# Trading the places of two weight loads in GpSimd's order, and dropping seven multiplied zero blocks

## The chip, the cores and the metric

The kernel runs on one core of one Trainium2 chip. The metric is the device time of one execution in microseconds (us), taken as the median of several runs. Engines are called as the profile calls them: PE (TensorE, matrix products), PEld (its weight loads), DVE (VectorE), ACT (ScalarE), POOL (GpSimd) and SP (SyncE, which here only issues DMAs).

## The reference, cut to what matters

```python
# attention: batch 4, 8 heads, 768 steps, head width 48
f = 1.0 / (1.0 + np.exp(-f_logit))
for t in range(S):
    state = f[:, :, t, :, None] * state + np.einsum('bhd,bhe->bhde', k[:, :, t], v[:, :, t])
    y[:, :, t] = np.einsum('bhd,bhde->bhe', q[:, :, t], state)
# its output, 3072 tokens of width 384, goes through a gated block of width 1536
gate = np.maximum(x @ w_gate, 0.0)
val = x @ w_val
return (gate * val @ w_out).astype(np.float32)
```

The inputs q, k, v, f_logit and the three weight matrices are f32; the output is f32.

## The kernel before

The recurrence is computed in chunks of 128 steps, six chunks for each of four batch entries. For a chunk, ACT makes exp and log of f_logit (`ef`, lines 478 and `ln`, 481), PE forms running sums of the logs (`cum`, lines 494 to 506), ACT turns those into factors (`ek` and `eq`, lines 516 and 518), and POOL or DVE multiply k and q with them (`hk`, `hq`, line 540). PE then makes the masked scores (`s`, line 650 in the first chunks; DVE masks them in `m`, line 657), the output of the chunk (`y`, line 672, and `yi`, line 708) and the new state (`kv`, line 695). ACT or DVE copy the output to `xT` (line 597), from where the gated block takes it: `g` and `u` (line 792) are the products with one slice of 128 columns of w_gate and of w_val, `r` (lines 797 and 798) is the maximum with 0, `p` (line 800) the product of both, and `o` (line 813) the product with w_out.

The weights come from memory as f32 and are cast to bf16 by DMAs that POOL issues (line 431). They come in slices: `wg2+2` holds columns 2 and 3 of w_gate (in units of 128 columns, called j), `wg0+2` columns 0 and 1, `wg4+4` and `wg8+4` four columns each; `wv...` the same of w_val, `wo...` row blocks of w_out. A two-column slice of w_gate or w_val has 384 rows of 1 KB in memory; `wo0+2` has 128 rows of 3 KB. The inputs q, k, v and f_logit are loaded by DMAs that SP and ACT issue (lines 406 and 411).

Every operation has a number. The table `ORDER` lists, by hand, for each engine the numbers in the order in which it issues them; each engine works strictly in that order, and waits for others by semaphores. Names such as `g00.1` mean operation `g`, chunk 0, batch place 0, slice 1; `cum13` is the running sum of chunk 1, place 3. Around the change these stand in the orders:

- PE: ... cum10 (232), cum11 (243), a filling, g00.1 (150), u00.1 (152), g00.0 (146), y02 (138), cum13 (279), cum12 (268), yi03 (142), u00.2 (156) ...
- POOL: ... hk01 (90), hq01 (91), wo0+2 (70), wv0+2 (52), sd10 (108), v02 (122), hq02 (117), hq03 (127), wg0+2 (51), wv2+2 (57), wg4+4 (62), wv4+4 (63) ...
- ACT: ... ef10, ln10, ef12 (266), r00.3 (159), ek10, eq11, dc10, eq10, r00.2 (155), ek11, ln12 (267), r00.0 (147), x02 (141), ek12 ...
- DVE: ... m031, sd11, m030, m020, m021 (135), r00.1 (151), p00.1 (153), x03 ...

An entry `~7512` in PE's list is a filling: 7 products of a zero tile, each 512 columns wide, whose results are overwritten (line 877). The number 60100 stands for 60 of width 100, and so on. A filling is written to the PSUM bank that the next operation opens, so that the wait for that bank's earlier reader (here r00.3 on ACT) stands ahead of the filling.

`HELD` gives some DMAs a wait that the data do not ask for: an entry `a: b` lets the load with number a start only when the load with number b has landed. Number 50 is `f0.2` (f_logit of the second unit of chunk 0), 53 is `k0.2`, 58 is `f1.0`. The waits for g00.1 are r00.3 (its PSUM bank) and the landing of wg0+2; for u00.1, m030 (its bank) and wv0+2; for g00.0, m020 (its bank); for y02, m021 and r00.2; for cum13, ln12; for o02.0, the first user of w_out, wo0+2 and wo2+2.

Of the kernel before, what the change touches and what calls it, by code (L numbers as in the profile page):

```python
# [22 lines left out]
ORDER = {  # L23
    "PE": [
        45, ~60100, 76, 87, ~4512, 84, ~3512, 92, 82, 103, ~2512, 94, 123, 112, 97, ~7512, 120, ~2512, 130, 102, 128, 106,
        118, 139, 158, 133, 154, 232, 243, ~7512, 150, 152, 146, 138, 279, 268, 142, 156, 160, 148, 174, 176, 170, 172, 186,
# [37 lines left out]
    ],  # L64
    "POOL": [
# [4 lines left out]
    ],  # L70
# [6 lines left out]
}  # L77

HELD = {
    51: 53, 57: 58, 59: 63, 63: 58, 65: 69, 67: 71, 70: 50, 71: 60, 72: 54, 517: 68,  # L80
}

BANKS = [
# [859 lines left out]
```

## Time and profile before

| | |
|---|---|
| median of 3 runs | 194.01 us (193.71 to 194.05) |
| the profiled execution: its own time | 193.82 us |
| its span, first to last instruction | 192.0 us |
| PE busy | 185.4 us |
| DVE busy | 146.3 us |
| ACT busy | 83.3 us |
| POOL busy | 59.8 us |
| granted clock of PE | 1.00 |

The span is the time between the first and the last instruction; the execution's own time has 1.8 us more around it. A row of a timeline gives the start, the duration, the engine, the source line, the operation and its tiles, how many instructions are merged in it, and in brackets how long the engine had been idle and what it then waited for. Instructions of one engine are pipelined, so the next one often starts a little before the duration of the one ahead is over. In a view of the DMA queues, q1 is the queue that SP fills and q0 the one that POOL fills; the columns are packets, megabytes and the time that the packets took as a share of the 16 DMA engines in that stretch. "DMA to landing" is the time from a DMA's issue until its last part has landed.

### The profile page before, as it was taken

The numbers are of one execution on the slowest core, as the hardware profiler recorded it, in microseconds if no ns is written. First come the engines' busy times: TensorE is split into PE (matmuls) and PEld (weight loads), VectorE is DVE, ScalarE is ACT, GpSimd is POOL, SyncE is SP. The second block draws the span as 40 slices with busy tenths as digits, with TensorE's granted clock in tenths as the row PEclk, the third lists the DMA queues.
The fourth block names the chain that finished last, engine by engine and source line by source line (L and its number), as shares of the span: only waits on it lengthen the run. The fifth ranks groups of instructions, "written<-read, shape, count | busy, mean of one in ns | idle before, by whom it ended". The sixth has DMA issues, their size and how long they took to land.

```text
span 192.0 us, 4872 instructions
## 1 busy us (share of the span) xinstructions
PE 185.4 (97%) x1992; PEld 110.1 (57%) x2010; DVE 146.3 (76%) x264; ACT 83.3 (43%) x183; POOL 59.8 (31%) x92
## 2 busy tenths in 40 slices
PE   7989999999999999999999999999999999999994
PEld 7556675565645556655555755556555555555553
DVE  4569946999868989879986789996888947677331
ACT  2776954520387780472214896613351220222211
POOL 8899320301055830358200273911180000000000
DMA  5999999999989997999989997991337010000413
GB/s 147 325 283 252 211 205 279 214 223 279 229 183 199 214 226 149 234 196 242 216 187 225 246 223 169 228 177 31 71 106 199 15 41 3 2 0 0 164 43 124
DMA packets 110311, 32.44 MB, mean 169 GB/s; under 512 B 103504, under 2 KB 110032, under 8 KB 110288
## 3 DMA queue, kind: packets, MB, share of 16 engines
q1 hardware_dynamic: 95120, 25.44, 59.7%
q0 software_dynamic: 3776, 3.54, 11.3%
q10 hardware_dynamic: 11392, 3.15, 7.2%
q8 instruction: 16, 0.26, 0.6%
q14 instruction: 7, 0.06, 0.1%
HBM read 25.95 MB, written 4.72 MB: 160 GB/s over the span
## 4 chain that ended last, share of the span: by engine, by line
PE 83%; DVE 5%; DMA 4%; ACT 3%; issue 1%; POOL 1%; SPq 1%; ACTq 0%
PE ps L792 43%; PE ps L813 25%; DMA f_in<-in_f_logit_dram 4%; PE ps L584 2%; DVE gT L800 2%; PE ps L745 2%; DVE hats L541 2%; PE ps L672 1%; PE ps L503 1%; PE ps L494 1%; POOL hats L540 1%; PE ps L772 1%; PE ps L650 1%; PE ps L756 1%; DVE qkT L556 1%
## 5 line engine op out<-in xcount | busy, mean ns | idle before, releaser
L800 DVE TENSOR_TENSOR gT<-relu,ps 128x512 bf16<-128x512 bf16 (+1 forms) x76 | 48.5, 655 | 15.4 <-PE ps L792 11.4
L792 PE MATMUL ps<-xT,wv 128*128 128x512 bf16 (+1 forms) x225 | 57.0, 368 | 0.3
L792 PE MATMUL ps<-xT,wg 128*128 128x512 bf16 (+1 forms) x216 | 55.2, 367 | 0.7 <-issue 0.2
L813 PE MATMUL ps<-wo,gT 128*128 128x384 bf16 (+2 forms) x300 | 51.9, 320 | 0.2 <-DVE gT L800 0.2
L797 ACT ACTIVATE relu<-ps 128x512 bf16<-128x512 f32 (+1 forms) x39 | 21.8, 565 | 48.5 <-PE ps L792 27.5
L813 PEld LDWEIGHTS ps<-wo,gT 128*128 128x128 bf16 x300 | 27.1, 98 | 18.4 <-DVE gT L800 1.2
L792 PEld LDWEIGHTS ps<-xT,wv 128*128 128x128 bf16 x228 | 23.6, 108 | 19.7 <-ACT expo L518 0.3
L792 PEld LDWEIGHTS ps<-xT,wg 128*128 128x128 bf16 x228 | 23.3, 108 | 18.8 <-ACT xT L597 0.3
L798 DVE TENSOR_SCALAR relu<-ps 128x512 bf16<-128x512 f32 (+1 forms) x37 | 24.9, 674 | 5.8 <-PE ps L792 4.8
L570 POOL CAST vpad<-v_in 128x384 bf16<-128x384 f32 x14 | 7.5, 549 | 43.7 <-PE ps L745 22.6
L592 DVE TENSOR_TENSOR ptm<-ps,tri 128x512 bf16<-128x512 f32 x32 | 19.9, 682 | 1.3 <-PE ps L584 1.3
L540 POOL TENSOR_TENSOR hats<-q_in,expo 128x384 bf16<-128x384 f32 x14 | 14.5, 1044 | 9.6 <-ACT expo L518 9.1
L540 POOL TENSOR_TENSOR hats<-k_in,expo 128x384 bf16<-128x384 f32 x13 | 13.8, 1071 | 6.5 <-ACT expo L516 3.7
L478 ACT ACTIVATE f_in<-f_in 128x768 f32<-128x768 f32 x12 | 10.1, 844 | 11.4 <-DMA f_in<-in_f_logit_dram 11.4
L456 POOL TENSOR_TENSOR st<-ssum,dec 128x384 bf16<-128x384 f32 x11 | 9.7, 878 | 17.1 <-DVE ssum L454 17.0
L518 ACT ACTIVATE expo<-ps 128x384 f32<-128x384 f32 x24 | 11.7, 491 | 4.1 <-PE ps L503 2.9
L597 ACT ACTIVATE xT<-ps 128x384 bf16<-128x384 f32 x10 | 5.4, 549 | 17.9 <-PE ps L672 8.6
L516 ACT ACTIVATE expo<-ps 128x384 f32<-128x384 f32 x24 | 11.5, 493 | 1.1 <-PE ps L494 0.6
L819 ACT ACTIVATE osb<-ps 128x384 f32<-128x384 f32 (+1 forms) x15 | 7.3, 484 | 10.4 <-PE ps L813 10.3
L877 PE MATMUL ps<-zeros 128*128 128x100 bf16 (+1 forms) x82 | 10.9, 311 | 0.4 <-issue 0.2
L657 DVE TENSOR_TENSOR ptm<-ps,tmask 128x512 bf16<-128x512 f32 x16 | 10.2, 682 | 1.4 <-PE ps L650 1.4
L481 ACT ACTIVATE bneg<-f_in 128x768 bf16<-128x768 f32 x12 | 10.1, 842 | 0.2
(78 smaller groups left out, 169.3 us busy)
## 6 DMA issues: line engine op xcount, KB each, us to landing
out_dram<-osb SPq DMA_DIRECT2D x23, 192.0 KB, 2.8
f_in<-in_f_logit_dram SPq DMA_DIRECT2D x11, 384.0 KB, 6.0
k_in<-in_k_dram SPq DMA_DIRECT2D x11, 384.0 KB, 5.6
q_in<-in_q_dram SPq DMA_DIRECT2D x10, 384.0 KB, 5.7
v_in<-in_v_dram SPq DMA_DIRECT2D x8, 384.0 KB, 4.9
v_in<-in_v_dram ACTq DMA_DIRECT2D x4, 384.0 KB, 6.1
q_in<-in_q_dram ACTq DMA_DIRECT2D x2, 384.0 KB, 7.1
wg<-in_moe_w_gate_dram POOLq DMA_DIRECT2D x2, 384.0 KB, 9.1
```

Of the source, the lines that this page charges most:

```text
L478: add(f"ef{c}{b0}", by("ACT", lambda: sc.activation(raw, raw, AF.Exp, scale=-1.0), act_(n)), keys, keys, key=P)
L516: add(f"ek{c}{b}", by("ACT", lambda: sc.activation(ex[:, 1, :], bc.ap[:, 0:HD], AF.Exp, scale=1.0), act_(HD)), [bc], [f"expk{ei}"], key=P + 1)
L518: add(f"eq{c}{b}", by("ACT", lambda: sc.activation(ex[:, 0, :], bc.ap[:, 0:HD], AF.Exp, scale=-1.0), act_(HD)), [bc], [f"expq{ei}"], key=P ...
L540: return {**by("POOL", lambda: gp.tensor_tensor(o, i_, e_, ALU.mult), pool_(HD)), **by("DVE", lambda: ve.tensor_tensor(o, i_, e_, ALU.mult ...
L592: add(f"m{c}{b}{j}", by("DVE", lambda b=b, j=j, mi=mi: ve.tensor_tensor(ptm[mi][:, j, :, :], s[b, j].ap[:, :].rearrange("p (n t) -> p n t" ...
L657: add(f"m{c}{b2[i]}{j}", by("DVE", lambda i=i, j=j, mask=mask: ve.tensor_tensor(ptm[mi[i]][:, j, :, :], s[j, i].ap[:, :].rearrange("p (n t ...
L792: z = te.matmul(bank.ap[:, 0:n], wt[:, kt, w_cols(j)], xT[xi][:, kt, n0:n1], start=(kt == 0), stop=(kt == NK - 1))
L797: add(f"r{c}{b0}.{j}", {**by("ACT", lambda: sc.activation(rdst, gate.ap[:, 0:n], AF.Relu), act_(n)), **by("DVE", lambda: ve.tensor_scalar_ ...
L798: **by("DVE", lambda: ve.tensor_scalar_max(rdst, gate.ap[:, 0:n], 0.0), dve_(n))}, [gate], [f"relu{ri}"], key=P)
L800: add(f"p{c}{b0}.{j}", by("DVE", lambda: ve.tensor_tensor(gT[gi][:, j, n0:n1], rdst, val.ap[:, 0:n], ALU.mult), dve_(n)), [val, f"relu{ri} ...
L813: z = te.matmul(o.ap[:, 0:e1 - e0], gT[gi][:, j, b * C:(b + 1) * C], wo[:, j, e0:e1], start=(j == 0), stop=(j == NJ - 1))
L877: te.matmul((op.opens[0].ap if op.opens else banks[7])[:, 0:fill % 1000], zeros[:, 0:128], zeros[:, 0:fill % 1000], start=True, stop=True, ...
```

## The change

Two numbers trade places in POOL's list, 70 (`wo0+2`) and 51 (`wg0+2`), and so do their entries in `HELD`: what is issued early waits for f0.2, what is issued late waits for k0.2, as before, but now it is wg0+2 that is issued early and wo0+2 that is issued late. The filling `~7512` ahead of 150 (`g00.1`) is taken out of PE's list. All other orders, waits and data are the same; g00.1 keeps its waits for r00.3 and for wg0+2.

```diff
 ORDER = {
     "PE": [
...
-        118, 139, 158, 133, 154, 232, 243, ~7512, 150, 152, 146, 138, 279, 268, 142, 156, 160, 148, 174, 176, 170, 172, 186,
+        118, 139, 158, 133, 154, 232, 243, 150, 152, 146, 138, 279, 268, 142, 156, 160, 148, 174, 176, 170, 172, 186,
...
     "POOL": [
-        25, 1, 36, 37, 38, 2, 4, 34, 11, 5, 20, 13, 7, 14, 8, 33, 26, 3, 39, 35, 16, 41, 17, 56, 40, 90, 91, 70, 52, 108,
-        122, 117, 127, 51, 57, 62, 63, 69, 68, 273, 71, 72, 73, 278, 264, 428, 420, 300, 392, 384, 395, 405, 393, 425, 418,
+        25, 1, 36, 37, 38, 2, 4, 34, 11, 5, 20, 13, 7, 14, 8, 33, 26, 3, 39, 35, 16, 41, 17, 56, 40, 90, 91, 51, 52, 108,
+        122, 117, 127, 70, 57, 62, 63, 69, 68, 273, 71, 72, 73, 278, 264, 428, 420, 300, 392, 384, 395, 405, 393, 425, 418,
...
 HELD = {
-    51: 53, 57: 58, 59: 63, 63: 58, 65: 69, 67: 71, 70: 50, 71: 60, 72: 54, 517: 68,
+    70: 53, 57: 58, 59: 63, 63: 58, 65: 69, 67: 71, 51: 50, 71: 60, 72: 54, 517: 68,
 }
```

## The prediction

> **What bounds the kernel now.** The page comes first: how full PE is, and which engine the chain that ended last runs through.
>
> ```profile
> span 192.0 us, 4872 instructions
> PE 185.4 (97%) x1992; PEld 110.1 (57%) x2010; DVE 146.3 (76%) x264; ACT 83.3 (43%) x183; POOL 59.8 (31%) x92
> PE 83%; DVE 5%; DMA 4%; ACT 3%; issue 1%; POOL 1%; SPq 1%; ACTq 0%
> ```
>
> PE sets the end, so whatever shortens PE's list shortens the kernel, provided that nothing else takes the place. The second view is the chain of waits in order of time, around the filling.
>
> ```profile
> 21.05 0.15 issue
> 21.20 1.46 PE ps L877 x6
> 22.66 0.98 PE ps L792 x9
> 23.64 0.66 PE ps L672 x62
> ```
>
> The filling (L877; six of its seven products are recorded) takes 1.46 us of the chain. Then PE works without a gap: g00.1, u00.1, g00.0 (nine products), y02 (L672). So at most 1.46 us can be won. Third, PE's own timeline there, with an earlier row (12.22) that shows how soon PE follows ACT:
>
> ```profile
> 12.22 0.82 PE L494 MATMUL ps<-bneg,tsum 128*128 128x384 bf16 x4 [0.20 <-ACT bneg L481]
> ...
> 22.49 0.49 PE L792 MATMUL ps<-xT,wg 128*128 128x256 bf16 x3
> 22.82 0.49 PE L792 MATMUL ps<-xT,wv 128*128 128x256 bf16 x3
> 23.15 0.49 PE L792 MATMUL ps<-xT,wg 128*128 128x256 bf16 x3
> 23.57 0.73 PE L672 MATMUL ps<-ptm,vpad 64*32 64x128 bf16 x64
> 24.24 0.82 PE L494 MATMUL ps<-bneg,tsum 128*128 128x384 bf16 x4
> ```
>
> Fourth, the two engines that feed these steps. First ACT's timeline (the row at 11.33 belongs to the earlier example), then DVE's.
>
> ```profile
> 11.33 0.83 ACT L481 ACTIVATE bneg<-f_in 128x768 bf16<-128x768 f32 x1
> ...
> 19.80 0.84 ACT L478 ACTIVATE f_in<-f_in 128x768 f32<-128x768 f32 x1 [0.40 <-DMA f_in<-in_f_logit_dram]
> 20.55 0.37 ACT L797 ACTIVATE relu<-ps 128x256 bf16<-128x256 f32 x1
> ...
> 22.32 0.38 ACT L797 ACTIVATE relu<-ps 128x256 bf16<-128x256 f32 x1
> 22.58 0.50 ACT L516 ACTIVATE expo<-ps 128x384 f32<-128x384 f32 x1
> 22.95 0.85 ACT L481 ACTIVATE bneg<-f_in 128x768 bf16<-128x768 f32 x1
> 23.69 0.39 ACT L797 ACTIVATE relu<-ps 128x256 bf16<-128x256 f32 x1
> 24.36 0.60 ACT L597 ACTIVATE xT<-ps 128x384 bf16<-128x384 f32 x1 [0.28 <-PE ps L672]
> ```
>
> ```profile
> 20.88 1.88 DVE L657 TENSOR_TENSOR ptm<-ps,tmask 128x512 bf16<-128x512 f32 x3
> ```
>
> This is the view that matters most. From 19.80 on ACT runs without a break until 24.08 (23.69 + 0.39): ef12, r00.3, the factors, r00.2, ek11, ln12, r00.0. Only its start is outside its own list: the landing of f1.2 at 19.80. And ln12, which ends at 22.95 + 0.85 = 23.80, is what cum13 needs; in the kernel before PE comes to cum13 at 24.24 and finds it ready. ACT is thus 0.4 us behind the filling, hidden by it.
>
> **The change part by part.** *The wait for wg0+2.* These rows give its issue, its landing and POOL's timeline:
>
> ```profile
> L431 POOL DMA_DIRECT2D wg<-in_moe_w_gate_dram x1: 815/815/815, 16.0 to 16.0; - x1
> ...
> DMA to landing us min/median/max: 6.0/6.0/6.0
> ```
>
> ```profile
> 11.17 0.59 POOL L431 DMA_DIRECT2D wo<-in_moe_w_out_dram  x1
> 11.76 0.75 POOL L431 DMA_DIRECT2D wv<-in_moe_w_val_dram  x1
> ...
> 14.12 1.95 POOL L540 TENSOR_TENSOR hats<-q_in,expo 128x384 bf16<-128x384 f32 x2 [0.30 <-ACT expo L518]
> 16.01 0.81 POOL L431 DMA_DIRECT2D wg<-in_moe_w_gate_dram  x1
> ```
>
> It lands at 16.0 + 6.0 = 22.0, and the filling covers that. Issued at 11.17 instead, it lands at 17.2, and has 4 us to spare until 21.2. That wait is gone.
>
> *The cost on POOL.* Issuing wg takes 0.81 us against 0.59 us for wo, so everything up to hq02 comes 0.22 us later; hq02 had 0.30 us of idle time ahead of it, waiting for ACT. Cost nothing, with 0.08 us to spare; without that cover, it would push the two `hq` that PE's transposes wait for by 0.22 us at most. After 16.01 the later weight loads are issued 0.22 us sooner, which nothing on PE waits for. wo0+2, now issued at 16.0, has until the first product with w_out:
>
> ```profile
> 41.33 0.81 PE L813 MATMUL ps<-wo,gT 128*128 128x384 bf16 x4
> ```
>
> *What PE meets without the filling.* r00.3 ends at 20.92 and g00.1 starts where the filling did, 21.20, done 0.33 us later (22.49 to 22.82). The three masks end about 21.5, 22.1 and 22.76 (20.88 + 1.88, in thirds). u00.1 needs the first: about 21.6. g00.0 needs the second: about 22.2. y02 needs the third: about 22.85, and it takes 0.67 us (23.57 to 24.24), to 23.52. Then cum13 needs ln12: 23.80 and the 0.06 us that PE followed ACT by at 12.22 (11.33 + 0.83 = 12.16), so 23.86 instead of 24.24. So even if nothing else moved, of 1.46 us only 0.38 us remain: the stall goes from the zeros to the masks (some 0.6 us in two waits) and to ln12 (0.34 us).
>
> *What the new order does to f1.2.* The 384 rows of wg0+2, where wo0+2 has 128, now go out on q0 beside f1.2, whose landing starts ACT's run. Here are its landing (the maximum is f1.2: 10.2 + 9.6 = 19.8) and the DMA queues in four stretches: 14 to 16 us (wo0+2 on q0), its part 14.5 to 15, 16 to 18 (wv0+2) and 18 to 19 (q1 nearly alone).
>
> ```profile
> L406 SPq DMA_DIRECT2D f_in<-in_f_logit_dram x2: 2096/2219/2342, 7.8 to 10.2; - x2
> ...
> DMA to landing us min/median/max: 8.6/9.1/9.6
> ```
>
> ```profile
> q1 hardware_dynamic: 876, 0.33, 62.1%
> q0 software_dynamic: 141, 0.19, 52.5%
> ...
> q1 hardware_dynamic: 240, 0.09, 64.6%
> q0 software_dynamic: 34, 0.05, 57.2%
> ...
> q0 software_dynamic: 391, 0.20, 71.2%
> q1 hardware_dynamic: 601, 0.23, 56.6%
> ...
> q1 hardware_dynamic: 828, 0.31, 113.6%
> ```
>
> Alone, q1 moves 828 packets in 1 us. Beside wo0+2 it moved 876 in 2 us, so the slice cost it (1656 - 876) / 828 = 0.94 us. Beside wv0+2 it moved 601: (1656 - 601) / 828 = 1.27 us. wg0+2 has the same rows as wv0+2, so exchanging it for wo0+2 ahead of f1.2 costs f1.2 about 0.33 us. The bounds: 0, since both slices write the same amount (0.19 and 0.20 MB in these stretches); and 0.48 us, if wo's price is scaled from the half microsecond in which it alone was on q0: (414 - 240) / 828 = 0.21 us for 34 of its 128 packets, 0.79 us for all, and 1.27 - 0.79 = 0.48. A gain isn't excluded either, and is rival C. I take 0.33, because the whole of both slices is in it.
>
> [...]
>
> *The sum.* f1.2 lands at 20.13, ACT's run moves with it, ln12 ends at 24.13, cum13 starts at 24.19 instead of 24.24: a gain of 0.05 us. With the bounds: cum13 at 23.86 to 24.34, a gain of 0.38 to a loss of 0.10. From there PE's list is as before and goes on as before, so the shift is carried to the end. The profiled execution took 193.82 us, 1.82 us more than its span; it becomes 193.77. The median of the runs is 0.19 above it, 194.01, and becomes 193.96.
>
> **The rivals.**
> - B, f1.2 doesn't move: 0.38 us less, 193.63. For it: equal bytes. Against it: 601 packets against 876.
> - C, f1.2 comes earlier: the wg slice takes 0.22 us longer to issue, so its packets may start later and let f1.2's pass; ACT then isn't what PE waits for, and y02 behind the third mask is. cum13 follows y02 at 23.52: 0.72 us less, 193.29. Against it: wo's first packets are there in the stretch 14.5 to 15, when f1.0, ahead of f1.2 on the same queue, hadn't landed yet (7.8 + 8.6 = 16.4), so much more than 0.22 us is needed.
> - The change does what its words say, the zeros' 1.46 us all come back: 192.55. Against it stand the masks and ln12, which no part of the change touches.
> - D, slower: f1.2's last part comes much later than the packet count says. It decides from 0.77 us on (0.38 us of room and 0.39 for a slowdown that can be told), and every tenth beyond is a tenth at the end: 1.0 us late gives 24.86 for cum13, 194.63. For it: the two f loads issued one behind the other took 8.6 and 9.6 us, so a landing can be a microsecond off. Against: the upper bound of 0.48.
> - E, slower: the zeros kept PE busy, and without them the clock falls. The rows of windows (PE busy is the second number with its count, the clock comes after POOL's):
>
> ```profile
> 12.00:12.50 0.50, 0.30 (x3) 0.21 (x3) 0.50 (x2) 0.17 (x1) 0.50 (x1) 1.00 1.31 200
> 21.00:24.30 3.30, 3.15 (x81) 2.12 (x82) 2.60 (x5) 3.06 (x9) 0.00 (x0) 1.00 1.28 204
> ```
>
>  [...] Against it: at 12 us PE stood at 0.30 of 0.50 with the clock at 1.00, and the new waits are 0.1 to 0.4 us each, with work between them. [...]
>
> **How the numbers follow.** The forecast, f1.2 some 0.2 to 0.5 us late and the gain eaten, has 0.52. B has 0.16, C 0.12, the full gain 0.02, D 0.12, E 0.06. What can be told from no change is about 0.2%, 0.39 us. C and the full gain are faster, and of B, which stands at that line, 0.05: 0.19. D and E are slower: 0.18. The rest, 0.63, is no difference. The predicted time is 194.0. The range goes down to C with a little for the runs' spread, 193.2, and up to D at 1.0 us late, 194.6; it leaves out E and the full gain. The forecast's own range is 193.6 to 194.2.
>
> **What would show it right or wrong.** Right: no L877 rows near 21; ACT's row of ef12 at about 20.1, still behind its DMA; cum13's row between 24.1 and 24.3, released by ACT's bneg. ef12 at 19.8 and cum13 at 23.86 is B; cum13 directly behind y02 at 23.5 is C; a clock under 1.00 is E. The step that I trust least is the 0.33 us: it is inferred from stretches with different neighbours, and if the landing of f1.2 follows something else than the packets ahead of it, the forecast is wrong by that.

## The result, and the profile after

| | time (median) | runs | ratio to the kernel before, 95% interval |
|---|---|---|---|
| kernel before | 193.94 us | 6 | |
| changed kernel | 195.02 us (194.77 to 195.22) | 6 | 1.0055 [1.0044, 1.0066] |

The change costs 1.08 us. The page of the changed kernel: its span, its engines, the packets of kind "instruction", and the chain by engine.

```profile
span 193.1 us, 4877 instructions
PE 185.7 (96%) x2003; PEld 109.1 (56%) x2003; DVE 146.2 (76%) x264; ACT 83.3 (43%) x183; POOL 60.2 (31%) x92
q8 instruction: 16, 0.26, 0.6%
PE 79%; DMA 5%; DVE 5%; SPq 5%; ACT 4%; issue 2%; ACTq 0%
```

"issue" is time in which an engine waited for nothing that the profile shows. Its step from 1% to 2% of the chain is little more than rounding (1.4% before, 1.5% after); what counts is one new piece of 1.14 us, which follows below. First, however, the place of the change. PE's timeline of the changed kernel around g00.1 (21.17), u00.1, g00.0, y02 (22.96) and cum13 (24.06):

```profile
21.17 0.50 PE L792 MATMUL ps<-xT,wg 128*128 128x256 bf16 x3
21.68 0.51 PE L792 MATMUL ps<-xT,wv 128*128 128x256 bf16 x3
22.28 0.50 PE L792 MATMUL ps<-xT,wg 128*128 128x256 bf16 x3
22.96 0.88 PE L672 MATMUL ps<-ptm,vpad 64*32 64x128 bf16 x64 [0.18 <-ACT relu L797]
24.06 0.82 PE L494 MATMUL ps<-bneg,tsum 128*128 128x384 bf16 x4 [0.21 <-ACT bneg L481]
```

And ACT's timeline of it, ef12 and ln12:

```profile
20.00 0.84 ACT L478 ACTIVATE f_in<-f_in 128x768 f32<-128x768 f32 x1 [0.53 <-DMA f_in<-in_f_logit_dram]
...
23.15 0.85 ACT L481 ACTIVATE bneg<-f_in 128x768 bf16<-128x768 f32 x1
```

Here all went much as foreseen: the wait for wg0+2 is gone, f1.2 lands 0.20 us later, ACT's unbroken run moves with it, and cum13 follows ln12 at 24.06, 0.18 us earlier than before. PE keeps this lead for 26 us. It loses it at one place, in yi13 (L708). PE's timeline there, the changed kernel and then the kernel before:

```profile
49.19 1.47 PE L813 MATMUL ps<-wo,gT 128*128 128x384 bf16 x8
50.59 0.29 PE L708 MATMUL ps<-qkT,st 128*32 128x128 bf16 x8
52.02 0.24 PE L708 MATMUL ps<-qkT,st 128*32 128x128 bf16 x4 [1.14 <-issue]
52.20 0.51 PE L695 MATMUL ps<-vpad,hats 64*128 64x96 bf16 x16
```

```profile
49.37 1.47 PE L813 MATMUL ps<-wo,gT 128*128 128x384 bf16 x8
50.78 0.35 PE L708 MATMUL ps<-qkT,st 128*32 128x128 bf16 x12
51.06 0.51 PE L695 MATMUL ps<-vpad,hats 64*128 64x96 bf16 x16
```

Before, yi13's twelve products run in one piece. Now eight run, then PE stands still for 1.14 us, and then the other four run, in the middle of one operation whose only wait lies ahead of its first product. The lead of 0.19 us (50.78 - 50.59) is a lag of 1.14 us (52.20 - 51.06) behind it: 1.33 us lost. The lag is still 1.1 us at the end (193.1 - 192.0). The windows view of 50.6 to 52.1 shows that no other engine was at work that PE could have waited for: DVE is busy for 0.14 us of it, ACT and POOL not at all; the changed kernel first, then the kernel before (the columns are the length, then PE, PEld, DVE, ACT and POOL busy, the clock, the DMA share and GB/s):

```profile
50.60:52.10 1.50, 0.36 (x13) 0.19 (x12) 0.14 (x1) 0.00 (x0) 0.00 (x0) 1.00 1.26 271
```

```profile
50.60:52.10 1.50, 1.50 (x34) 0.85 (x32) 0.81 (x2) 0.73 (x2) 0.00 (x0) 1.00 1.23 312
```

The clock stands at 1.00. What did happen just ahead of the gap stands in the view of the DMA queues: an "instruction" packet of 16 KB, the fifth of the sixteen. In the changed kernel it starts in the stretch 49 to 50.6 us, beside a busy queue q10; in the kernel before the packet of the same number starts in 45.5 to 47 us, beside busy queues too (q1 92.4%, q10 31.1%).

```profile
q10 hardware_dynamic: 1771, 0.34, 132.4%
q8 instruction: 1, 0.02, 5.1%
```

```profile
q8 instruction: 1, 0.02, 5.4%
```

Either packet took 1.3 us (5.1% of 16 engines in 1.6 us, 5.4% in 1.5 us): it was not slower in the changed kernel, it came later, at 49.39 instead of 46.71 us.

So the first theory, F, which this profile doesn't show and the runs below test: these packets bring PE's program, in blocks of 16 KB. The zeros were not only 1.46 us of work but also fourteen instructions, seven products and seven weight loads. Without them, by F, all of PE's later code lies fourteen instructions sooner with respect to the blocks, and one block is asked for so late that PE runs out of instructions in yi13.

### The profile page after: what moved, and what is told of

Same layout as the page of the kernel before. It is cut to its first block, busy times and chain, and to the rows that moved or that the text cites. A ratio compares the mean times of both kernels' runs of the same rounds, so it can differ in the third digit from the quotient of the medians.

```text
span 193.1 us, 4877 instructions
## 1 busy us (share of the span) xinstructions
PE 185.7 (96%) x2003; PEld 109.1 (56%) x2003; DVE 146.2 (76%) x264; ACT 83.3 (43%) x183; POOL 60.2 (31%) x92
## 4 chain that ended last, share of the span: by engine, by line
PE 79%; DMA 5%; DVE 5%; SPq 5%; ACT 4%; issue 2%; ACTq 0%
PE ps L792 43%; PE ps L813 25%; DMA f_in<-in_f_logit_dram 5%; SPq L406 5%; PE ps L584 2%; DVE gT L800 2%; PE ps L745 2%; DVE hats L541 2%; PE ps L503 1%; PE ps L772 1%; ACT expo L518 1%; ACT relu L797 1%; PE ps L756 1%; DVE qkT L556 1%; PE ps L752 1%
## 5 line engine op out<-in xcount | busy, mean ns | idle before, releaser
L800 DVE TENSOR_TENSOR gT<-relu,ps 128x512 bf16<-128x512 bf16 (+1 forms) x76 | 48.5, 654 | 15.4 <-PE ps L792 11.4
L792 PE MATMUL ps<-xT,wg 128*128 128x512 bf16 (+1 forms) x228 | 57.8, 368 | 0.1
L820 DVE COPY osb<-ps 128x384 f32<-128x384 f32 (+1 forms) x10 | 5.3, 526 | 6.4 <-PE ps L813 4.2
## 6 DMA issues: line engine op xcount, KB each, us to landing
out_dram<-osb SPq DMA_DIRECT2D x23, 192.0 KB, 2.2
```

What stands on the lines that cost most here:

```text
L792: z = te.matmul(bank.ap[:, 0:n], wt[:, kt, w_cols(j)], xT[xi][:, kt, n0:n1], start=(kt == 0), stop=(kt == NK - 1))
L800: add(f"p{c}{b0}.{j}", by("DVE", lambda: ve.tensor_tensor(gT[gi][:, j, n0:n1], rdst, val.ap[:, 0:n], ALU.mult), dve_(n)), [val, f"relu{ri} ...
```

## The experiments

The ratios are to runs of the kernel before on the same chip, whose medians in the three groups were 193.91, 193.89 and 193.89 us. A `~7002` is a filling of seven products of zeros, each 2 columns wide: fourteen instructions, next to no work (its row in the first of these runs takes 0.33 us, that of the wide filling 1.46). Long lines of `ORDER` are cut, marked by "...". It writes to a bank that the next operation overwrites.

**Seven narrow products in the place of the seven wide ones.**

```diff
-        118, 139, 158, 133, 154, 232, 243, 150, 152, 146, 138, ...
+        118, 139, 158, 133, 154, 232, 243, ~7002, 150, 152, 146, 138, ...
```

> The changed kernel with seven products of zeros put back where the seven were taken out, each 2 columns wide instead of 512: PE's program is as long as before, its time there is not. Theory F (the seven products and their seven weight loads held PE's program in place against the 16 KB blocks in which it is fetched; without them a block is fetched too late and PE has nothing to issue for 1.1 to 1.3 us at 50.7): the gap in L708 near 50.7 is gone, cum13 still starts at 24.06, and the time is 0.2 us under the kernel before, 193.7 to 193.8. Rival S (the loads that trade places shift later DMAs, and the gap comes from that): the gap stays, 195.0. Rival Z (the work of the zeros mattered, for the clock or the pace): 195.0, as 14 columns are next to no work.

Measured: 193.53 us (193.23 to 194.11 in 11 runs), ratio 0.9987 [0.9978, 0.9997]. The gap is gone; yi13 runs in one piece, in the slowest of these executions, the profiled one:

```profile
51.03 0.35 PE L708 MATMUL ps<-qkT,st 128*32 128x128 bf16 x12
```

The same loads, the same waits at 21 us, no work of zeros worth the name, and 1.5 us less than the changed kernel. S and Z both fall. Two details were off: the time is some 0.2 us under the one expected, and cum13 came at 24.49 in this profile, as f1.2 landed at 20.4.

**The same seven, behind the gap.**

```diff
-        217, 302, 314, 304, ...
+        217, ~7002, 302, 314, 304, ...
```

> The changed kernel with the same seven 2-column products put ahead of g10.0, behind the gap (55.1 us in the changed kernel's profile). Theory F: the code ahead of the gap lies as in the changed kernel, so the gap near 50.7 stays, 195.0 (up to 0.2 more for the products themselves). If the mere number of PE's instructions mattered and not their place, it would be 193.8.

Measured: 194.95 us, 1.0055 [1.0039, 1.0070]. The gap is where it was, behind the eighth product:

```profile
50.84 0.29 PE L708 MATMUL ps<-qkT,st 128*32 128x128 bf16 x8
52.39 0.24 PE L708 MATMUL ps<-qkT,st 128*32 128x128 bf16 x4 [1.25 <-issue]
```

Not the number of instructions counts, but whether they lie ahead of the place.

**The two halves of the change alone.** First the loads traded and the wide filling kept.

```diff
-        118, 139, 158, 133, 154, 232, 243, 150, 152, 146, 138, ...
+        118, 139, 158, 133, 154, 232, 243, ~7512, 150, 152, 146, 138, ...
```

> The two loads trade places, the filling of seven products of 512 columns stays. Theory F: no gap at 50.7; f1.2 lands at 20.0 instead of 19.8, so r00.3 and with it the filling come 0.2 us later and so does cum13, 24.4: 0.2 us over the kernel before, 194.1. Rival S: the gap is there, 195 to 195.5.

Measured: 194.05 us, 1.0004 [0.9995, 1.0013], no gap. The filling, held by r00.3, which f1.2 makes late, starts at 21.62 instead of 21.20, and cum13 comes at 24.66, later than the 24.4 expected:

```profile
21.62 1.46 PE L877 MATMUL ps<-zeros 128*128 128x512 bf16 x6 [0.74 <-ACT relu L797]
```

Then the filling taken out of the kernel before, the loads as they were.

```diff
-        118, 139, 158, 133, 154, 232, 243, ~7512, 150, 152, 146, 138, ...
+        118, 139, 158, 133, 154, 232, 243, 150, 152, 146, 138, ...
```

> The kernel before without the filling, the loads as before. Theory F: g00.1 waits for wg0+2 until 22.0 and cum13 comes at 23.95, 0.3 us early; then the gap of 1.1 to 1.3 us near 50.7: 194.8 to 195.1. Rival S: no gap, 193.6 to 193.7.

Measured: 195.02 us, 1.0060 [1.0046, 1.0074]: the whole loss, without the trade.

```profile
22.35 0.49 PE L792 MATMUL ps<-xT,wg 128*128 128x256 bf16 x3 [1.33 <-DMA wg<-in_moe_w_gate_dram]
...
52.07 0.24 PE L708 MATMUL ps<-qkT,st 128*32 128x128 bf16 x4 [1.15 <-issue]
```

PE waits openly for wg0+2 now, cum13 comes at 24.09 (23.95 was expected), and nevertheless the loss comes at 52.07. The trade of the loads neither causes the loss nor prevents it.

**The old loads with the narrow filling.**

```diff
-        118, 139, 158, 133, 154, 232, 243, ~7512, 150, 152, 146, 138, ...
+        118, 139, 158, 133, 154, 232, 243, ~7002, 150, 152, 146, 138, ...
```

> The kernel before with its filling narrowed from 512 to 2 columns; the loads stand as before. Theory F: no gap near 50.7. g00.1 waits for wg0+2 until about 22.3 as without any filling, and cum13 comes at 24.1: 193.7 to 193.8, much as with the loads traded, so the trade itself is worth next to nothing. If the trade of the loads is what made the kernel with narrow filling faster: 193.9 to 194.0.

Measured: 193.75 us (193.38 to 195.19 in 12 runs), 0.9997 [0.9983, 1.0011], no gap in the profile. One of the twelve took 195.19, as long as the kernels with the gap; whether it had it isn't known, as it has no trace (its granted clock was 0.991, where the other eleven had 0.998 or more). The interval separates this kernel neither from the one before nor from the one with the loads traded.

**How many instructions it takes.** The changed kernel with three, fourteen and one narrow products in the place of the seven.

```diff
-        118, 139, 158, 133, 154, 232, 243, 150, 152, 146, 138, ...
+        118, 139, 158, 133, 154, 232, 243, ~3002, 150, 152, 146, 138, ...
```

> The changed kernel with three 2-column products (six instructions) where seven of 512 columns stood. Theory F says that it depends on where the code lies: either the block still comes too late, and the gap then cuts into yi13 three products sooner, behind 5 of its 12 instead of 8, at 195.0; or six instructions are enough to bring its request forward, and there is no gap, 193.5 to 193.9. A gap that stays behind the 8th product would speak against F.

Measured: 193.55 us, 0.9991 [0.9981, 1.0000], no gap.

```diff
-        118, 139, 158, 133, 154, 232, 243, 150, 152, 146, 138, ...
+        118, 139, 158, 133, 154, 232, 243, ~14002, 150, 152, 146, 138, ...
```

> The changed kernel with fourteen 2-column products, 14 instructions more than the kernel before has there. Theory F: the blocks' borders lie still further ahead in the work, the request for the one behind 50 comes as early as before, no gap near 50.7, 193.5 to 193.9. If only the exact length of the old program was free of the gap: 195.

Measured: 193.71 us, 0.9994 [0.9984, 1.0004], no gap.

```diff
-        118, 139, 158, 133, 154, 232, 243, 150, 152, 146, 138, ...
+        118, 139, 158, 133, 154, 232, 243, ~1002, 150, 152, 146, 138, ...
```

The next expectation speaks of theory W, which is told in full further down: PE's reading of its program asks for the late block at a certain place, and a wait ahead of that place holds the request.

> The changed kernel with one 2-column product (two instructions) ahead of g00.1, where three were enough. Theory W: the place of the request moves by two instructions; either the gap is gone, 193.4 to 193.9, or it stays and cuts into yi13 behind 7 of 12 products, 195.0. Both in different runs would say that the border lies just there.

Measured: 194.84 us, 1.0047 [1.0022, 1.0072]. The gap cuts one product sooner:

```profile
50.65 0.29 PE L708 MATMUL ps<-qkT,st 128*32 128x128 bf16 x7
52.08 0.27 PE L708 MATMUL ps<-qkT,st 128*32 128x128 bf16 x5 [1.14 <-issue]
```

Each product more ahead of the gap, with its weight load, cuts yi13 one product sooner, as it must if a border fixed in the program is what PE stops at. The traces let one count to that border. The windows view from the start of the span to 51.6 us, which lies inside the gap, has PE's products and weight loads up to there as its first two counts; the changed kernel, the one with three narrow products behind y12 (below) and the one with one narrow product:

```profile
0.00:51.60 51.60, 47.52 (x727) 30.87 (x727) 39.00 (x94) 25.64 (x54) 22.24 (x48) 1.00 1.15 240
```

```profile
0.00:51.60 51.60, 47.36 (x727) 30.66 (x727) 39.15 (x94) 25.65 (x54) 22.22 (x48) 1.00 1.15 240
```

```profile
0.00:51.60 51.60, 46.80 (x727) 30.53 (x728) 39.20 (x94) 25.67 (x54) 22.24 (x48) 1.00 1.15 239
```

In all five kernels with the gap PE stops behind its weight load 727 or 728, whichever product of yi13 that belongs to. But from two added instructions to six the cut does not just move on a little; the whole gap is gone, and with seven narrow products the packet stands in the stretch 45.5 to 47 again. If F holds, something between asks for the block, and it stands near a long wait.

**What holds the request.** In PE's order y12 comes shortly ahead of yi13 and cannot start before DVE's mask m111 is done. The rows of DVE (m111 is the second of the two) and of PE in the changed kernel:

```profile
46.79 1.29 DVE L657 TENSOR_TENSOR ptm<-ps,tmask 128x512 bf16<-128x512 f32 x2 [0.26 <-PE ps L650]
```

```profile
46.67 1.47 PE L813 MATMUL ps<-wo,gT 128*128 128x384 bf16 x8
48.08 0.74 PE L672 MATMUL ps<-ptm,vpad 64*32 64x128 bf16 x64
```

The mask ends at 48.08 and y12 starts at 48.08. Theory W puts the place of the request just behind that wait. Three narrow products on either side of y12 tell it apart from a mere count. Ahead of it:

```diff
-        ... 221, 210, 211, 253, 212, 227, 294, 295, 222, ...
+        ... 221, 210, 211, ~3002, 253, 212, 227, 294, 295, 222, ...
```

> The changed kernel with three 2-column products ahead of s10 (46.1 us), that is ahead of y12, which PE cannot start before 48.1, when DVE's mask is done. Theory W (the block that comes too late is asked for when PE's instruction reading passes a certain place in the program; in the changed kernel this place lies just behind y12's wait, so the request is held until 48.1, in the kernel before just ahead of it): six instructions ahead of y12 push that place in front of the wait, the block's fetch is seen near 46.5, no gap, 193.4 to 193.9. Rival K (six instructions help wherever they stand ahead of the gap): the same here. Rival N (it is the narrow products at 21 us that help, by their wait there): the gap stays, 195.0.

Measured: 193.69 us, 0.9996 [0.9984, 1.0007]. No gap (yi13 in one piece), and the packet stands in 47 to 48.5:

```profile
q8 instruction: 1, 0.02, 5.3%
```

```profile
50.55 0.35 PE L708 MATMUL ps<-qkT,st 128*32 128x128 bf16 x12
```

Behind it:

```diff
-        ... 221, 210, 211, 253, 212, 227, 294, 295, 222, ...
+        ... 221, 210, 211, 253, 212, 227, 294, ~3002, 295, 222, ...
```

> The changed kernel with the same three 2-column products behind y12, ahead of kv12 (48.7 us), still ahead of the gap. Theory W: the place of the request stays behind y12's wait, the fetch is seen near 49.4 as in the changed kernel, and the gap stays, now behind some 5 of yi13's 12 products instead of 8, as the block's border lies six instructions sooner in the work: 195.0. Rival K: no gap, 193.4 to 193.9.

Measured: 195.14 us, 1.0059 [1.0037, 1.0082]. The packet stands in 49 to 50.6, and the gap cuts three products sooner than in the changed kernel:

```profile
q8 instruction: 1, 0.02, 4.9%
```

```profile
50.69 0.28 PE L708 MATMUL ps<-qkT,st 128*32 128x128 bf16 x5
51.92 0.29 PE L708 MATMUL ps<-qkT,st 128*32 128x128 bf16 x7 [0.95 <-issue]
```

The same six instructions help ahead of y12 and not behind it. K and N fall, W stands. The packets' starts in the traces say the same of all thirteen kernels: in the eight without the gap the fifth packet starts at 46.25 to 47.46 us, ahead of y12 (47.90 to 48.68); in the five with it, at 49.16 to 49.56, which is 1.15 to 1.32 us behind the start of y12. And the count narrows down the place of the request that W supposes: with 631 or 632 weight loads ahead of y12 the packet comes late, with 634 or more it doesn't, so by W the place lies 93 to 95 weight loads, with their products some 190 instructions, ahead of the stop.

**The price of a slice ahead of f1.2.** The kernel before with the narrow filling, and wo0+2 taken from ahead of wv0+2 to behind wg8+4.

```diff
-        ... 90, 91, 70, 52, 108, 122, 117, 127, 51, 57, 62, 63, 69, 68, 273, ...
+        ... 90, 91, 52, 108, 122, 117, 127, 51, 57, 62, 63, 69, 68, 70, 273, ...
```

> The kernel before with its filling narrowed to 2 columns and wo0+2 taken from ahead of wv0+2 and put behind wg8+4 in POOL's order, so that no slice but wv0+2 is on q0 ahead of f1.2's landing. By the packets (a slice of w_out cost q1 0.94 us), f1.2 lands at 18.9 instead of 19.8; ACT starts at 19.4, when ln10 is done. wg0+2 is then what PE waits for, at 21.5 to 22.0, and cum13 comes between 23.6 and 23.9: 193.3 to 193.6. If f1.2's landing does not depend on what is on q0, it stays at 19.8 and the time is that of the narrow filling with the old order.

Measured: 193.47 us (193.23 to 194.25 in 12 runs), 0.9989 [0.9980, 0.9999]. The DMA's and ACT's rows of this kernel (f1.2 is the load issued at 10.3):

```profile
L406 SPq DMA_DIRECT2D f_in<-in_f_logit_dram x2: 2342/2525/2708, 7.9 to 10.3; - x2
...
DMA to landing us min/median/max: 8.6/8.7/8.8
```

```profile
19.39 0.83 ACT L478 ACTIVATE f_in<-f_in 128x768 f32<-128x768 f32 x1
```

f1.2 lands at 18.9 (10.3 + 8.6, f1.2's own time in the trace), as the packets say, and ef12 no longer waits for it. This kernel and the one with seven narrow products and the traded loads are the two whose intervals just stay below 1: some 0.1% faster than the kernel before, hardly more than the noise.

## Why the prediction was wrong

*The wait for wg0+2*, right. wg0+2 landed at 17.6 (17.2 was said), and g00.1 starts at 21.17 without a DMA wait.

*The cost on POOL*, right: nothing of it is seen on PE. hq02 started at 14.12 before and at 14.18 after, and POOL's operation at 9.90, ahead of the change, was already 0.08 us late. Only the later weight loads did not come 0.22 us sooner (16.83 against 16.82), which nothing on PE waits for.

*What PE meets without the filling*, right in place and size but for one wait: u00.1 and g00.0 wait for the masks and cum13 for ln12, but y02 starts at 22.96 behind r00.2 on ACT, which ends at 22.89, where the third mask ends at 22.82. ACT's run was 0.20 us later, and so r00.2 was the last to come.

*f1.2*, too large in size, and the reason given for it isn't confirmed: 0.33 us was said, and ACT's start moved by 0.20 us in the profiled pair. Over all profiles, ef12 starts at 20.08 on average in the nine kernels that have wg0+2 ahead (19.88 to 20.43), and at 19.88 in the three that have wo0+2 there (19.80 to 20.01): again 0.20 us, with a spread in each group that is as large or larger. The trace also has the arrival of each of the load's sixteen parts. Fifteen of them are in by 18.75 us in the kernel before and by 18.89 in the changed one, and on average by 18.78 in the three kernels and by 18.80 in the nine (18.38 to 19.05); it is the last part, 1.0 to 2.0 us behind the others, that starts ACT, and why it lags no run shows. So the bulk of the load shows no clear price of the trade. The whole price of a slice of w_out, 0.94 us by the packets, fits better: in its absence f1.2 landed 0.9 us sooner, its first fifteen parts 1.1 us.

*The sum* is the step that failed, in the sentence "From there PE's list is as before and goes on as before, so the shift is carried to the end". Up to 50.6 us that holds: a lead of 0.18 us against 0.05 foreseen. Then the gap takes 1.33 us, and a lag of 1.1 us is what is carried to the end. The filling had been costed as time alone; that it was also fourteen instructions of PE's program, and that without them the fifth instruction packet starts at 49.39 us instead of 46.71, had no term. The page of before did show sixteen "instruction" packets of 0.26 MB in all, and they were passed over.

*The rivals.* None had this mechanism. D (f1.2 far later) is refuted by ACT's row at 20.00, E (the clock) by 1.00 through the gap, with PE busy for 0.36 of 1.50 us, and by the narrow products, which do next to no work and bring the time back; the lowest mean clock of any execution here is 0.991. C and the full gain are refuted by cum13 waiting for ACT at 24.06. The kernel with the traded loads and the narrow filling is 0.38 us under the kernel before, just B's number, but that is luck as far as its trace shows: in the profiled execution f1.2 did not stay at 19.8, it landed at 20.4.

The range ended at 194.6, and the time is 195.02.

What stays open: what exactly asks for a block, and why PE goes on only 1.3 to 1.6 us after the late packet's time is over. The runs show that the packet starts ahead of y12 where 634 or more weight loads stand ahead of y12's wait, and 1.15 to 1.32 us behind y12's start where 631 or 632 do; they don't show the request itself. That the packets are PE's program is inferred: the gap comes behind the same count of PE's instructions in all five kernels that have it, and none of the eight with the packet ahead of y12 has a gap.

## What to carry to other kernels

Here fourteen instructions taken out of a long unrolled program moved the start of an instruction packet from 46.71 to 49.39 us, and PE stood still for 1.14 us, some 30 us behind the edit. By theory W one block's request fell behind a wait; PE then went through 96 weight loads and their products (727 - 631) in 2.8 us (48.08 to 50.88) and stopped. When an edit shows its local effect and the time still goes the other way, look for idle time put down to "issue" inside an operation, and for an instruction packet just ahead of it. A handful of near-empty instructions ahead of the place tells it apart; here two instructions did not mend it and six did. Taking out a filler's work and taking out its instructions are two edits: try both.

## What the runs showed of the hardware

Sixteen instruction packets came in the kernel before and in the changed one, 0.26 MB in all, so 16 KB each. The fifth took 1.3 us in either. PE stood still for 0.95 to 1.25 us where it came late, in all five kernels with the late packet and in none of the other eight. In the kernel before no idle time of PE put down to "issue" is over 0.19 us; in the changed kernel one is, the gap of 1.14 us. By theory W and the count above, the request for that block stands some 190 recorded instructions ahead of the stop, and y12's wait, which ended at 48.08 us, held it.

The landing of one load of 384 KB decided where ACT's run began, and from one kernel to the next with the same loads ahead of it it varied by half a microsecond (ef12 at 19.88 to 20.43), more than the trade of the loads was worth. In every profile one of the load's sixteen parts came 1.0 to 2.0 us behind the other fifteen, and in all profiles but that of the kernel with wo0+2 taken back it was what ACT waited for.
